# Gated attention and MLP mixer on one core: when the loads of batch 0 are issued

## The chip, the cores and the metric

The kernel runs on one core of one Trainium2 chip. The metric is the device time of one execution in microseconds. Seven runs of the kernel before took 1146.55 to 1149.58 us, with a median of 1147.07 us.

## What is computed

The sizes are 8 batches, 3008 rows, 256 columns, z with 64 columns, and an MLP mixer with 256 token features and 1536 channel features.

```python
scores = matmul(z, z.T) / S
attn   = maximum(scores, 0) ** 2
x      = u * matmul(attn, v)                     # gated attention

h  = maximum(x.T @ w_tok1, 0) @ w_tok2           # token mixing
u2 = x + h.T
out = u2 + maximum(u2 @ w_ch1, 0) @ w_ch2        # channel mixing
```

u, v, z and the weights come as float32; the kernel casts them to bfloat16 while it loads them.

## The kernel before

**Tiling.** The 3008 rows are cut into 6 groups of 512 (NG = NQ = 6; the last one holds 448). A block (b, q, g) is the scores of query group q against key group g of batch b, as four tiles of 128 keys. For a block, PE makes the scores in two units of two tiles (`score_run`, L424), ACT takes relu with the factor 1/S from PSUM into an `at` buffer (`relu`, L462), and DVE squares it there (`square`, L470). PE then multiplies v with it (`av_matmul`, L646) into two accumulators. A row is all six blocks of one q. At its end the accumulator is summed (ACT L771, DVE L777) and gated with u (DVE L798), which gives x.

**Symmetry.** The scores are symmetric, so from batch 1 on only the blocks with g >= q are computed. The block (q, g) gives (g, q) through a transpose by DMA, which SP issues (`flip`, L518, `fl<-at`). In batch 0 all blocks are computed directly, and no flip is made. There are six `at` buffers and ten `fl` buffers; the v tiles of batch 0 live in `fl` buffers too.

**Mixer.** When a batch's last row is done, its mixer is queued: `tok1` (L851), `tok2` (L870), `ch1` (L911, with w_ch1), `ch2` (L955, with w_ch2). PE does these pieces between the attention rows of the next batch. So batch 0's mixer runs in batch 1, and the weights are loaded once, before it.

**Order.** The order of every engine's instructions is made when the program is built: a planner keeps a clock for PE (`pe[0]`) and for the other engines with a cost for each operation, and picks what PE does next (scores, AV or a mixer piece) by what is ready on that clock. A load counts as ready at a time that is written beside it: `w_done[part].t` for the channel weights (L1214), `tok2_done` for w_tok2. The engines run their lists in this order and wait for one another through semaphores.

**Loads.** Loads that cast are issued by POOL: v (`load_v`, L206), u (`load_u`, L218), z (`load_z`, L125), w_tok1 (`load_w_tok1`, L236), w_tok2 (`load_w_tok2`, L246), w_ch1 and w_ch2 (`load_w_ch`, L253 and L258; two parts each). SP issues the transposes of u (L228), z (L137), x (L811) and of the flips, and the stores. `at_group(n, f)` puts f ahead of step n of the attention, a step being one block of a row; batch 0 has the steps 0 to 35, batch 1 the steps 36 to 71. In batch 0 the u and z loads have steps of their own. The other loads that the later work needs are in the list `items` (v of batch 1, w_tok1, w_tok2, w_ch), spread evenly over the steps from 7 on (L1227, L1228).

**Marks.** From batch 1 on, loads go through `ask`, which issues at most one in 4.5 us and puts a tiny POOL copy ahead of it: `after(recent[0])` (L120) copies one column of the newest tile that was squared, evacuated or summed on the planner's clock into `mark`. POOL does its list in order, so the load waits until that tile is there. In batch 0 no such copy stands ahead of the items: POOL issues them as fast as its queue lets it, except where a u load waits for its buffer.

Of the kernel before, what the change touches and what calls it, by code (L numbers as in the profile page):

```python
# [55 lines left out]
def kernel(  # L56
# [22 lines left out]
    NQ = (S + QW - 1) // QW  # L79
    NG = KT // GK  # L80
# [37 lines left out]
    def after(column):  # L118

        nc.gpsimd.tensor_copy(mark[:column.shape[0], :1], column)  # L120
# [77 lines left out]
    def load_v(b, c):  # L198
        if b == 0:

            vt = sb.tile([P, GK, D], BF16, tag="fl", name="v_sb", bufs=ROOM["fl"])
            live["fl"] += 1
        else:
            vt = sb.tile([P, GK, D], BF16, tag="v", name="v_sb", bufs=8)
        n = full_tiles[c]
        nc.gpsimd.dma_start(out=vt[:, :n, :], in_=rows_of(v[b], c))  # L206
        if n < GK:
            for r in range(2):
                nc.gpsimd.dma_start(
                    out=vt[r * TAIL:(r + 1) * TAIL, n, :], in_=last_rows(v[b]))  # L210
        vs[b, c] = vt
        v_in[b, c] = Done(pe[0] + 9.0 if b > 1 else 0.0)
        loading(LOAD)
# [37 lines left out]
    def load_w_ch(part):  # L251
        if part < 2:
            nc.gpsimd.dma_start(  # L253
                out=w_ch1_sb[:, part, :], in_=moe_w_ch1[part * P:(part + 1) * P, :])
        else:
            h = CHT // 2
            c0 = (part - 2) * h
            nc.gpsimd.dma_start(  # L258
                out=w_ch2_sb[:, c0:c0 + h, :],
                in_=moe_w_ch2.rearrange("(cc c) d -> c cc d", c=P)[:, c0:c0 + h, :])  # L260
        loading(LOAD * 1.5)
# [99 lines left out]
    pe = [0.0]  # L361
# [750 lines left out]
    def at_group(n, f):  # L1112
        fetch.setdefault(n, []).append(f)
# [3 lines left out]
    recent = [None]  # L1117
# [91 lines left out]
    w_done = [Done() for _ in range(4)]  # L1209
    tok2_done = [Done() for _ in range(NG)]  # L1210

    def ask_w_ch(part):
        load_w_ch(part)
        w_done[part].t = pe[0] + 16.0  # L1214


    W_LATER = 4

    def ask_w_tok2(c):
        load_w_tok2(c)  # L1220
        tok2_done[c].t = pe[0] + 10.0

    items = [lambda c=c: load_v(1, c) for c in vorder]
    items += [lambda c=c: load_w_tok1(c) for c in range(NG)]
    items += [lambda c=c: ask_w_tok2(c) for c in range(NG)]
    items += [lambda part=part: ask_w_ch(part) for part in range(4)]
    for k, item in enumerate(items):  # L1227
        at_group(NG + 1 + k * (NQ * NG - 2 * NG + W_LATER) // len(items), item)  # L1228

    per_batch = 0.87 * NQ * (2 + CHT // 2) + 1.35 * 4 * NQ  # L1230
    flat = NQ * NG * 1.73 + NQ * (NQ + 1) / 2 * 0.44
# [172 lines left out]
```

## Time and profile before

The profiled execution took 1147.9 us; its span, from the first to the last instruction, is 1146.1 us.

| Engine | busy us | share of the span |
|---|---|---|
| PE (matmul) | 1133.5 | 99% |
| PE (weight load) | 672.6 | 59% |
| DVE | 637.9 | 56% |
| ACT | 549.0 | 48% |
| POOL | 154.0 | 13% |

Where things stand in the span, by the timeline: attention of batch 0 to about 90 us, with the first 25 us as start-up; rows 0 and 1 of batch 1 from 89.7 to 112.9 us; tok1 of batch 0 from 112.9 us; rows 2 and 3 of batch 1 from 118.2 to 141.4 us; then the rest of batch 0's mixer (tok2 from 141.4, ch1 from 144.0, ch2 from 153.5 us) and rows 4 and 5 from 188.7 us on. The items are issued by POOL at 18.5 us (v) to 76.2 us (the last of w_ch).

How to read the profile: busy time of PE has modelled ends, so its pace is better read from the starts of matmuls. A timeline row has the start, the length, the engine, line and operation, the tiles (written, then read), the number of instructions merged, and in brackets the idle time ahead and what ended it. In a row of windows, the numbers in front of (x...) are the busy times of PE, PE's weight loads, DVE, ACT and POOL; behind them stand the granted clock, the share of the DMA engines and the GB/s. q0 is the queue of POOL's loads, q1 that of SP's DMAs.

### The profile page before, as it was taken

The page shows a single profiled execution, that of the slowest core. Times are in us where ns is not written, and L with a number is a line of the kernel's source. Part 1 is how long each engine was busy: PE and PEld are TensorE (multiplying, and loading weights), DVE is VectorE, ACT ScalarE, POOL GpSimd, SP SyncE. Part 2 cuts the span into 40 slices and gives each one's busy share as a digit, 9 for nine tenths or more (in the row PEclk, how much of TensorE's full clock was granted, in tenths as well). Part 3 has the DMA queues.
Part 4 walks back from the last instruction along what each step waited for, and adds up shares of the span by engine and source line. Part 5 has one row for each costly group of instructions (what it writes and reads, how often), then busy time and mean ns, then how long its engine had stood idle before and what let it go on. Part 6 is the DMA issues. An engine that isn't in the chain of part 4 may idle for free.

```text
span 1146.1 us, 22411 instructions
## 1 busy us (share of the span) xinstructions
PE 1133.5 (99%) x9160; PEld 672.6 (59%) x9219; DVE 637.9 (56%) x947; ACT 549.0 (48%) x699; POOL 154.0 (13%) x387
## 2 busy tenths in 40 slices
PE   8999999999999999999999999999999999999998
PEld 3455465645557566565565655665566655566666
DVE  6888454465553755537545375555644646434544
ACT  7999534374352752526525354345542554422331
POOL 3600110210111001111011100211002110000000
PEclk9999999999999999999999999999999999999999
DMA  9999954985879858899688986798967999642122
GB/s 162 178 175 237 160 120 99 193 147 118 169 121 204 160 111 157 133 196 176 109 154 135 189 174 115 150 157 174 158 128 145 169 129 177 121 102 56 51 84 65
DMA packets 468199, 164.85 MB, mean 144 GB/s; under 512 B 431936, under 2 KB 445824, under 8 KB 468096
## 3 DMA queue, kind: packets, MB, share of 16 engines
q1 hardware_dynamic: 440240, 130.72, 58.7%
q0 software_dynamic: 27344, 32.32, 20.6%
q8 instruction: 72, 1.18, 0.4%
q10 hardware_dynamic: 512, 0.38, 0.1%
q14 instruction: 31, 0.25, 0.1%
HBM read 65.40 MB, written 24.64 MB: 79 GB/s over the span
## 4 chain that ended last, share of the span: by engine, by line
PE 96%; DMA 3%; issue 0%; POOL 0%; DVE 0%; ACT 0%; SPq 0%; ACTq 0%; DVEq 0%
PE acc L646 40%; PE op L955 21%; PE hp L911 21%; PE sc L424 6%; PE a_ps L851 4%; PE h_ps L870 4%; DMA v_sb<-in_v_dram 1%; DMA fl<-at 1%; DMA zf<-in_z_dram 1%; DMA at<-at 0%; DVE h2pre L927 0%; POOL v_sb L206 0%; ACT at L462 0%; PE first_acc L563 0%; SPq L159 0%
## 5 line engine op out<-in xcount | busy, mean ns | idle before, releaser
L646 PEld LDWEIGHTS <-v_sb 64*128 64x128 bf16 x4418 | 238.8, 94 | 223.1 <-issue 4.3
L646 PE MATMUL acc<-at,v_sb 64*128 64x512 bf16 (+1 forms) x2738 | 341.8, 374 | 0.2
L925 ACT ACTIVATE h2pre<-hp 128x1024 bf16<-128x1024 f32 (+1 forms) x161 | 160.8, 1000 | 313.9 <-PE hp L911 313.6
L462 ACT ACTIVATE at<-sc 128x1024 bf16<-128x1024 f32 (+1 forms) x294 | 287.9, 1027 | 34.0 <-PE sc L424 26.7
L911 PE MATMUL hp<-xT,w_ch_sb 128*128 128x512 bf16 (+1 forms) x1106 | 254.9, 374 | 2.4
L470 DVE TENSOR_TENSOR at<-at 128x1024 bf16<-128x1024 bf16 (+1 forms) x294 | 200.6, 687 | 101.7 <-ACT at L462 98.2
L955 PE MATMUL op<-w_ch_sb,h2pre 128*128 128x256 bf16 x2208 | 251.4, 273 | 1.3 <-ACT at L462 1.0
L955 PEld LDWEIGHTS <-h2pre 128*128 128x128 bf16 x2208 | 215.4, 98 | 39.0 <-issue 3.2
L927 DVE TENSOR_SCALAR h2pre<-hp 128x1024 bf16<-128x1024 f32 (+1 forms) x127 | 153.8, 1211 | 91.6 <-PE hp L911 91.6
L646 PE MATMUL acc<-fl,v_sb 64*128 64x512 bf16 (+1 forms) x1680 | 195.0, 367 | 0.0
L911 PEld LDWEIGHTS <-w_ch_sb 128*128 128x128 bf16 x1152 | 111.8, 98 | 125.7 <-issue 4.4
L971 DVE TENSOR_TENSOR res<-op,u_sb 128x512 f32<-128x512 f32 x87 | 60.2, 691 | 153.0 <-PE op L955 152.8
L424 PE MATMUL sc<-zT 64*128 64x512 bf16 (+1 forms) x732 | 132.2, 360 | 0.2 <-ACT zT L1237 0.2
L777 DVE TENSOR_TENSOR cp<-acc,cp 128x512 f32<-128x512 f32 (+1 forms) x94 | 63.4, 675 | 101.7 <-ACT cp L771 100.6
L771 ACT COPY cp<-acc 128x512 f32<-128x512 f32 (+1 forms) x89 | 51.5, 579 | 131.2 <-PE acc L646 115.1
L450 ACT ACTIVATE at<-sc 128x512 bf16<-128x512 f32 (+3 forms) x144 | 52.1, 440 | 54.4 <-PE sc L424 53.7
L424 PEld LDWEIGHTS <-zT 64*128 64x128 bf16 x732 | 40.3, 94 | 42.2 <-issue 6.9
L798 DVE TENSOR_TENSOR xT<-cp,uT 128x512 bf16<-128x512 f32 (+1 forms) x94 | 62.4, 665 | 3.1 <-PE hp L911 1.4
L879 DVE TENSOR_TENSOR xT<-xT,h_ps 128x1024 bf16<-128x1024 bf16 (+1 forms) x48 | 55.6, 1172 | 8.6 <-PE h_ps L870 8.3
L120 POOL CAST mark<-at 128x1 f32<-128x1 bf16 x49 | 13.2, 269 | 339.4 <-DVE at L470 339.4
L499 DVE TENSOR_TENSOR at<-at 128x512 bf16<-128x512 bf16 (+3 forms) x144 | 38.1, 320 | 30.1 <-ACT at L450 28.1
L932 POOL COPY hs<-h2pre 128x128 bf16<-128x128 bf16 x48 | 15.7, 326 | 253.6 <-ACT h2pre L925 234.0
(56 smaller groups left out, 341.1 us busy)
## 6 DMA issues: line engine op xcount, KB each, us to landing
out_dram<-res SPq DMA_DIRECT2D x87, 256.0 KB, 2.3
v_sb<-in_v_dram POOLq DMA_DIRECT2D x40, 256.0 KB, 6.0
ur<-in_u_dram POOLq DMA_DIRECT2D x40, 256.0 KB, 5.2
w_tok_sb<-in_moe_w_tok_dram POOLq DMA_DIRECT2D x10, 256.0 KB, 9.3
zs<-in_z_dram POOLq DMA_DIRECT2D x35, 64.0 KB, 3.3
at<-at SPq DMA_TRANSPOSE x108, 2.4
fl<-at SPq DMA_TRANSPOSE x105, 5.3
v_sb<-in_v_dram POOLq DMA_DIRECT2D x8, 192.0 KB, 4.6
```

What stands on the lines that cost most here:

```text
L424: nc.tensor.matmul(sc[:, r, c0:c1], zT[h, k:k + P], zT[h, m + c0:m + c1], start=True, stop=True)
L462: nc.scalar.activation(view, sv, ACT.Relu, scale=inv_S)
L470: nc.vector.tensor_mul(view, view, view)
L646: nc.tensor.matmul(o, vs[blk.b, g][rows, i, dh * P:(dh + 1) * P], rhs, start=(dh, h) not in blk.begun, stop=stop, skip_group_check=True)
L777: nc.vector.tensor_add(cp[:, :W], acc[:, 0, :W], cp[:, :W])
L798: nc.vector.tensor_mul(xT[:, dh, :full * P].rearrange("p (t s) -> p t s", s=P), acc[:, :full * P].rearrange("p (t s) -> p t s", s=P), uT[: ...
L879: nc.vector.tensor_add(to, to, h[:, :, :n * P].rearrange("p h (s t) -> p h t s", t=n))
L911: nc.tensor.matmul(hp[:, r, :W], w_ch1_sb[:, dc, cc * P:(cc + 1) * P], xT[:, dc, :W], start=(dc == 0), stop=(dc == DT - 1))
L925: nc.scalar.activation(h2[:, :, :W], hp[:, :, :W], ACT.Relu)
L927: nc.vector.tensor_single_scalar(h2[:, :, :W], hp[:, :, :W], 0.0, AX.max)
L955: nc.tensor.matmul(op[:, i, :], h2, w_ch2_sb[:, cc, :], start=(cc == 0 and (i == 0 or apart)), stop=(cc == CHT - 1), skip_group_check=True)
L971: nc.vector.tensor_add(res.rearrange("p i (h d) -> p i h d", d=P), op.rearrange("p i (h d) -> p i h d", d=P), us[:, :, half * 2:half * 2 + ...
```

## The change

Two things change. The items of batch 0 now each have a mark ahead of them (`when_reached`), where a newest tile is known. And the four loads of channel weights leave the list and go to the steps 46, 48, 51 and 53, which are in batch 1, with a mark as well. With 18 items left instead of 22, the even spread over batch 0 has other steps: v at 7 to 14, w_tok1 at 16 to 23, w_tok2 at 25 to 32. The planner's time from issue to readiness of channel weights goes from 16 to 10 us.

```diff
     def ask_w_ch(part):
         load_w_ch(part)
-        w_done[part].t = pe[0] + 16.0
+        w_done[part].t = pe[0] + 10.0
 
-    W_LATER = 4
+    W_LATER = 3
 
     items = [lambda c=c: load_v(1, c) for c in vorder]
     items += [lambda c=c: load_w_tok1(c) for c in range(NG)]
     items += [lambda c=c: ask_w_tok2(c) for c in range(NG)]
-    items += [lambda part=part: ask_w_ch(part) for part in range(4)]
+    def when_reached(item):
+        if recent[0] is not None:
+            after(recent[0])
+        item()
+
     for k, item in enumerate(items):
-        at_group(NG + 1 + k * (NQ * NG - 2 * NG + W_LATER) // len(items), item)
+        at_group(NG + 1 + k * (NQ * NG - 2 * NG + W_LATER) // len(items),
+                 lambda item=item: when_reached(item))
+
+    for part, group in enumerate((46, 48, 51, 53)):
+        at_group(group, lambda part=part: when_reached(lambda: ask_w_ch(part)))
```

## The prediction

> **What bounds the kernel now.** I read the page first. Its opening rows say that PE is busy for 99% of the span. Ends of matmuls are modelled, so that alone is weak.
>
> ```profile
> span 1146.1 us, 22411 instructions
> PE 1133.5 (99%) x9160; PEld 672.6 (59%) x9219; DVE 637.9 (56%) x947; ACT 549.0 (48%) x699; POOL 154.0 (13%) x387
> ```
>
> Next the windows (length; busy time of PE, PEld, DVE, ACT, POOL; clock; DMA share; GB/s), cut where the change acts: batch 0 behind its start-up, the first four query rows of batch 1, the rest of batch 1.
>
> ```profile
> 20.00:90.00 70.00, 69.91 (x647) 36.02 (x648) 59.90 (x96) 65.07 (x73) 21.93 (x40) 1.00 1.18 179
> 90.00:144.00 54.00, 53.95 (x487) 27.94 (x483) 34.09 (x54) 37.94 (x43) 5.40 (x13) 1.00 1.04 194
> 144.00:260.00 116.00, 115.68 (x914) 69.04 (x920) 63.73 (x90) 54.89 (x67) 15.34 (x40) 1.00 0.77 140
> ```
>
> PE lacks 0.09, 0.05 and 0.32 us. The timeline of PE tests the pace by starts, not by ends:
>
> ```profile
> 98.31 1.04 PE L646 MATMUL acc<-at,v_sb 64*128 64x512 bf16 x8
> 99.17 0.40 PE L424 MATMUL sc<-zT 64*128 64x512 bf16 x2
> 99.38 1.04 PE L646 MATMUL acc<-at,v_sb 64*128 64x512 bf16 x8
> ```
>
> Ten half-height matmuls run as five pairs from 98.31 to 99.38, so one pair in 0.214 us; the planner's own figure for 512 columns (`column_time`) is 0.216. Nothing hides between the starts. The view of waits for PE names no wait at all from 24 to 260 us and 1.2 us in the rest. So the loads of batch 0, crowded as they are, cost TensorE nothing. A change of their time has about 0.5 us to win here; the 3.55 us that PE lacks in the first 24 us lie ahead of the first moved instruction.
>
> **What the change does to the program.** I compared the built instruction orders of both kernels. PE, DVE and ACT have the same instructions in the same order, so the planner's changed numbers (16 to 10 us for the channel weights, the spacing of the loads) move no matmul. POOL gets 22 more copies into `mark` and its loads in another order; SP swaps one pair of transposes in batch 1 (the turn of u goes ahead of the turn of x). PE's work is therefore unchanged, and the change can act only through a wait.
>
> **Part 1, 18 marks and loads in batch 0.** Before, POOL ran ahead of the compute until its queue or a u buffer stopped it:
>
> ```profile
> 40.29 2.12 POOL L236 DMA_DIRECT2D w_tok_sb<-in_moe_w_tok_dram  x4 [3.02 <-DMA v_sb<-in_v_dram]
> ...
> 55.77 0.57 POOL L253 DMA_DIRECT2D w_ch_sb<-in_moe_w_ch_dram  x1
> ...
> 75.39 1.67 POOL L258 DMA_DIRECT2D w_ch_sb<-in_moe_w_ch_dram  x2
> ```
>
> After, each load stands behind a mark of the newest squared score block. I dated each mark by the end of the square that it names, in the trace of before: the v loads of batch 1 leave at about 27 to 41 us, w_tok1 at 46 to 58, w_tok2 at 62 to 80. Needed: v at 89.7 us (first AV of batch 1), w_tok1 at 112.9, w_tok2 at 141.4. With the longest landing of each in the trace (15.5 us for v, 13.2 for the token weights) they are there by 57, 72 and 94 us: over 30 us early. Cost 0. Without that cover the first of them would stop PE for its lateness.
>
> Queued behind the marks on POOL are the u and z loads and the memset of xT. The z loads of batch 1 leave by 36 us, as before (34); SP begins to turn them at 42.6 behind the x of row 1, so nothing moves. u(1,1) leaves at about 75, as before (74.87). The memset moves from 77 to about 81; its xT is written at 88.4. Cost 0.
>
> The marks themselves: POOL's `mark` copies are 0.27 us in the mean and 0.19 at least, so 22 are 4 to 6 us of an engine that is idle 87% of the time. Here a rule speaks against the change. The Trainium skill ("SBUF — State Buffer", section "SBUF: two separate sides") says that a VectorE instruction with both inputs in SBUF and a GpSimd instruction that reads SBUF take a shared port as a lock, and the later one waits for the whole of the other. L470 squares `at` in SBUF, so by the rule every mark may push a square back by 0.2 to 0.6 us, together 4 to 13 us of DVE. The rows: DVE is idle for 10.1 of the 70 us, squares stay near 0.69 us beside the marks of batch 1, and it is the mark that stretches (0.51 to 0.58 instead of 0.19 us). From 30 us on a square ends over 1 us before PE takes it, so 0.2 us later costs nothing. By the rule taken at its worst, with a push of 0.6 us at the few PSUM slots that DVE frees with under 0.5 us in hand, at most 1 us. I take 0.
>
> **Part 2, relief.** From 75 to 88 us the two w_ch2 loads and SP's transposes shared the DMA engines, and the transposes of u landed 11.5 us behind their issue (2.7 when alone). That made SP late for the first flips of batch 1. After, the w_ch2 loads are gone from there, and the flips up to 109 us land perhaps 3 us earlier. The tightest user is ACT at 96.36 us: it overwrites an `at` buffer whose flip landed at 95.94, with 0.4 us in hand. It was not late, so the gain is 0; it only gets slack.
>
> **Part 3, the four channel loads in batch 1.** By the same dating they leave at about 109, 119, 124.5 and 126.5 us. First users: w_ch1 at 144.03 (L911), w_ch2 at 153.45 (L955).
>
> ```profile
> DMA to landing us min/median/max: 9.4/13.1/15.3
> ```
>
> Even 15.3 us behind the last issues gives 134 and 142: 10 and 11 us early. The skill's fit in "DMA: Bandwidth & Descriptors", section "Anatomy of one DMA" (2.0 us plus the bytes at 436 GB/s), makes 2.9 us of a load of 384 KB, and would say that it disturbs nobody for longer than that. The trace has 5.2 us for a u load of 256 KB, where the fit has 2.6, so I take the trace, with 15.3 as the upper end.
>
> The price lies elsewhere: in SP's transposes, which share the engines. From 52 to 64 us (queue, packets, MB, share):
>
> ```profile
> q0 software_dynamic: 1712, 1.73, 91.8%
> q1 hardware_dynamic: 1717, 0.42, 31.2%
> ```
>
> and from 96 to 104 us, without loads:
>
> ```profile
> q1 hardware_dynamic: 8403, 2.11, 119.3%
> ```
>
> Transposes alone make 1050 packets per us; beside loads 143, one for each packet of a load. So a load nearly stops them while it moves. How long: landings that follow one another are 1.7 us apart for w_ch1 (70.32, 71.98) and 3.1 for w_ch2 (84.76, 87.82). The flips that this hits, from SP's timeline:
>
> ```profile
> 108.73 8.25 SPq L518 DMA_TRANSPOSE fl<-at  x4
> 117.08 1.41 SPq L811 DMA_TRANSPOSE x_sb<-xT  x1
> 118.61 1.75 SPq L228 DMA_TRANSPOSE uT<-ur  x1
> 122.75 14.01 SPq L518 DMA_TRANSPOSE fl<-at  x3
> ```
>
> PE reads these flips late (batch 1's row 4 starts at 189 us). What hurries is ACT, which waits for a flip before it reuses the `at` buffer. From landing to that use I find 7.0, 6.6, 8.7 and 7.5 us for the four flips from 108.73 on, and 3.0 us for the one issued at 122.75 (landed 128.44, ACT at 131.44). The first w_ch1 load adds 1.7 us to the four, the second 1.7 to the tail of them, x and uT: covered. The flip of 122.75 is released by PE, which frees its buffer at 122.55, so an earlier SP doesn't help it. Its packets moved behind those of the u load issued at 122.11, from 125.3 to 128. The third channel load begins to move at about 126.2 (an estimate: its issue plus 1.7 us, as for that u load). About 900 of the flip's 2048 packets are through by then; the other 1150 go at about one for one, 250 in a us: 4.6 us instead of 1.1, landing at about 131.9. ACT comes to it at 131.44, and the PE matmul that takes the PSUM slot behind it has 0.3 us in hand.
>
> ```profile
> 131.44 1.73 ACT L462 ACTIVATE at<-sc 128x896 bf16<-128x896 f32 x2
> ```
>
> So PE stalls 0 to 1 us; I take 0.5. Ends: 0 if the flip is through before the load moves, 3.2 us if both w_ch2 loads pass in front of it (2 x 3.1 less 3.0). What is late next is nothing: after 134 us ACT idles until 139.75 and the next flips are for 189 us.
>
> **Sum.** Profiled execution: span 1146.1 + 1.8 around it = 1147.9. Parts 1 and 2: 0; part 3: +0.5. That gives 1148.4 on its scale. It lies 0.8 above the median of the runs (1147.07), so 1147.6 as a median.
>
> **The rivals.** *Late flips (slower).* The flip issued at 122.75 stands behind both w_ch2 loads, or the w_ch1 loads delay SP so that it isn't issued in time. It decides when the flip lands over 3.3 us later than before. Then ACT at L462, the scores and PE stop for the excess: 1.5 to 5 us, 1149 to 1152, say 1150. For it: transposes fell to a seventh of their pace beside loads. Against: 3.0 us of slack, and half of the flip is out early. Chance 0.20.
>
> *Late weights (slower).* A channel load slips past 144 or 153 us. It would take 25 us from issue to landing, against 15.3 at most; 1150 to 1157. Chance 0.04.
>
> *Relief pays (faster).* Fewer collisions in batch 0 let PE run better: bounded by the 0.5 us that PE lacks from 20 to 260 us, so 1146.6; more only if the start-up moved. Chance 0.06.
>
> *The cover holds* (forecast, 1147.1 to 1148.5): 0.70.
>
> **Chances.** A measurement of this kernel tells about 0.2% (2.3 us) from no change. Forecast: 0.69 within, 0.01 slower. Late flips: 0.05 within, 0.15 slower. Late weights: 0.04 slower. Relief: 0.04 within, 0.02 faster. Sums: 0.02, 0.78, 0.20. The range goes from the relief to the late flips short of their worst: 1146.2 to 1150.6.
>
> **What would show it.** Right: PE waits for nothing from 20 to 125 us; POOL's marks in batch 0 follow L470; w_ch landings lie before 144 and 153 us; ACT L462 waits for `fl<-at` by 1 us at most near 131 us. Wrong: an idle PE ahead of L424 or L646 between 96 and 135 us behind ACT and `fl<-at` (late flips), PEld L911 or L955 behind w_ch (late weights), squares well over 0.69 us beside marks (the lock), or a shorter start-up.

## The result and the profile after

The changed kernel takes 1156.72 us (median of 12 runs, 1155.31 to 1163.04). The kernel before took 1147.28 us beside it (30 runs, 1146.13 to 1151.79). The ratio is 1.0086 (95% interval 1.0075 to 1.0097): 9.4 us slower, where 0.5 us more was forecast and 1150.6 us was the upper end. The profiled execution took 1157.85 us. Medians and ranges here and below are of all runs; ratios and their intervals are of the runs in the fast state alone (within 1.5% of a kernel's fastest run), so the two need not agree to the last digit.

The opening rows of its page:

```profile
span 1156.1 us, 22453 instructions
PE 1136.9 (98%) x9160; PEld 674.7 (58%) x9219; DVE 638.5 (55%) x947; ACT 549.0 (47%) x699; POOL 161.6 (14%) x409
```

The span grew by 10.0 us, but PE's busy time by 3.4 only: most of the loss is PE standing still. The windows tell where, cut as before (length; busy time of PE, PEld, DVE, ACT, POOL; clock; DMA share; GB/s):

```profile
20.00:90.00 70.00, 69.92 (x645) 36.09 (x646) 59.72 (x96) 65.22 (x73) 26.58 (x54) 1.00 1.04 161
90.00:144.00 54.00, 45.29 (x410) 24.18 (x408) 31.83 (x50) 36.81 (x41) 8.91 (x22) 0.93 1.18 188
144.00:260.00 116.00, 115.68 (x914) 67.53 (x918) 57.41 (x81) 50.04 (x62) 14.46 (x39) 0.99 0.73 138
```

In batch 0, where 18 marks were added, PE lacks 0.08 us of 70 (before: 0.09). From 90 to 144 us it lacks 8.71 instead of 0.05, and the clock row drops from 1.00 to 0.93. It is one stop, by the timeline of PE:

```profile
132.31 1.03 PE L646 MATMUL acc<-fl,v_sb 64*128 64x512 bf16 x8
142.05 1.89 PE L646 MATMUL acc<-at,v_sb 64*128 64x512 bf16 x8 [8.71 <-ACT at L462]
...
145.41 3.84 PE L646 MATMUL acc<-at,v_sb 64*128 64x512 bf16 x30
...
152.64 2.76 PE L870 MATMUL h_ps<-w_tok_sb,a_sb 128*128 128x512 bf16 x11
```

The same matmuls before, where nothing stops them:

```profile
132.00 1.03 PE L646 MATMUL acc<-fl,v_sb 64*128 64x512 bf16 x8
132.86 1.03 PE L646 MATMUL acc<-at,v_sb 64*128 64x512 bf16 x8
...
141.37 2.76 PE L870 MATMUL h_ps<-w_tok_sb,a_sb 128*128 128x512 bf16 x11
```

In after, PE waits for ACT's relu of the last score tile of row 3. The eight matmuls behind the stop take 1.89 us instead of 1.03: PE came back at about half its pace. The timeline of ACT names what ACT waits for:

```profile
141.08 1.73 ACT L462 ACTIVATE at<-sc 128x896 bf16<-128x896 f32 x2 [9.22 <-DMA fl<-at]
```

It is the instruction that the prediction showed at 131.44, and it waits 9.22 us for the flip that frees its `at` buffer: the flip that was issued at 122.75 before. SP's own timeline tells when it was issued now (the length is SP's time for the issues, not the transfer):

```profile
109.24 12.79 SPq L518 DMA_TRANSPOSE fl<-at  x4
122.15 4.58 SPq L228 DMA_TRANSPOSE uT<-ur  x1
126.84 3.40 SPq L811 DMA_TRANSPOSE x_sb<-xT  x1
130.78 16.52 SPq L518 DMA_TRANSPOSE fl<-at  x3
```

The same four flips took SP 8.25 us before, and the turns of u and x 1.75 and 1.41. So SP reached the urgent flip at 130.78, 8.03 us late. The two w_ch1 loads stand in that stretch, issued by POOL at 108.50 and 119.82: the four flips took 4.5 us more beside the first, the turn of u 2.8 us more beside the second. The turn of x took another 2.0 us more, but beside a u load (issued at 122.51) and the first w_ch2 load: from 127 to 130 us the queue of the loads moved 700 packets and that of the transposes 270. What a load does to transposes is seen in the DMA view from 111 to 114 us (queue, packets, MB, share of 16 engines). Before, without a load:

```profile
q1 hardware_dynamic: 3031, 0.77, 115.1%
```

After, with the first w_ch1 load under way:

```profile
q0 software_dynamic: 117, 0.33, 81.9%
q1 hardware_dynamic: 227, 0.05, 9.0%
```

Transposes fell from 3031 packets to 227. The packets of the first w_ch1 load move from 110.7 to 114.3 us and those of the second from 121.8 to 125.3, and q1 has no packet at all in 111 to 113 and 122 to 124.

**Where the time went.** The flip is issued 8.03 us later, and takes 10.19 us to land (at 140.97) instead of 5.69, since the w_ch2 loads and two z loads move beside it. Together it is 12.5 us late, against 3.0 us of slack: PE starts again 8.88 us later relative to the matmuls ahead (9.74 us from start to start, 0.86 before). From there to the first tok2 matmul it needs 10.59 us instead of 8.51, so the half pace costs another 2.08. With 0.31 us of difference in the start-up that is 11.27 us at the tok2 matmul (152.64 against 141.37); about 1 us comes back later, where a wait of L955 for ACT of 1.0 us is gone. The span differs by 10.0.

### The profile page after: what moved, and what is told of

Read it like the earlier page. It is cut to its first block, busy times and chain, and to the rows that moved or that the text cites. A ratio compares the mean times of both kernels' runs of the same rounds, so it can differ in the third digit from the quotient of the medians.

```text
span 1156.1 us, 22453 instructions
## 1 busy us (share of the span) xinstructions
PE 1136.9 (98%) x9160; PEld 674.7 (58%) x9219; DVE 638.5 (55%) x947; ACT 549.0 (47%) x699; POOL 161.6 (14%) x409
## 4 chain that ended last, share of the span: by engine, by line
PE 97%; DMA 2%; issue 0%; DVE 0%; ACT 0%; SPq 0%; POOL 0%; ACTq 0%; DVEq 0%
PE acc L646 40%; PE op L955 21%; PE hp L911 21%; PE sc L424 6%; PE a_ps L851 4%; PE h_ps L870 4%; DMA fl<-at 1%; PE first_acc L563 1%; DMA zf<-in_z_dram 1%; DMA at<-at 0%; DMA v_sb<-in_v_dram 0%; DVE h2pre L927 0%; ACT at L462 0%; SPq L159 0%; PE up L1196 0%
## 5 line engine op out<-in xcount | busy, mean ns | idle before, releaser
L955 PE MATMUL op<-w_ch_sb,h2pre 128*128 128x256 bf16 x2208 | 251.4, 273 | 0.3 <-DVE h2pre L927 0.2
L955 PEld LDWEIGHTS <-h2pre 128*128 128x128 bf16 x2208 | 215.4, 98 | 37.9 <-issue 2.2
L777 DVE TENSOR_TENSOR cp<-acc,cp 128x512 f32<-128x512 f32 (+1 forms) x94 | 63.4, 675 | 103.3 <-ACT cp L771 102.2
L120 POOL CAST mark<-at 128x1 f32<-128x1 bf16 x70 | 21.9, 314 | 364.8 <-DVE at L470 364.8
L798 DVE TENSOR_TENSOR xT<-cp,uT 128x512 bf16<-128x512 f32 (+1 forms) x94 | 62.4, 665 | 3.1 <-PE hp L911 1.4
```

The lines of the kernel that those rows point to most:

```text
L777: nc.vector.tensor_add(cp[:, :W], acc[:, 0, :W], cp[:, :W])
L798: nc.vector.tensor_mul(xT[:, dh, :full * P].rearrange("p (t s) -> p t s", s=P), acc[:, :full * P].rearrange("p (t s) -> p t s", s=P), uT[: ...
L955: nc.tensor.matmul(op[:, i, :], h2, w_ch2_sb[:, cc, :], start=(cc == 0 and (i == 0 or apart)), stop=(cc == CHT - 1), skip_group_check=True)
```

## Experiments

The theory: channel loads in batch 1 stop SP's transposes, SP comes late to the urgent flip, ACT waits for its buffer, PE for ACT; all else of the change is free. Rivals: the marks cost; w_ch2 beside the flip is enough; w_ch1 is enough; SP's swapped pair of turns costs. Each kernel ran beside the kernel before (medians 1147.11 to 1147.50 us). The time of the profiled execution is named beside the median, since it is the one that is read.

### Marks alone

The kernel before, with a mark ahead of all 22 items, channel loads among them:

```diff
-    for part, group in enumerate((46, 48, 51, 53)):
-        at_group(group, lambda part=part: when_reached(lambda: ask_w_ch(part)))
+    items += [lambda part=part: ask_w_ch(part) for part in range(4)]
```

(shown against after; the numbers 16 and W_LATER = 4 are those of before)

> All 22 items of batch 0 get a mark, the four channel loads among them; they stay in batch 0 (at the steps of the kernel before). Theory (channel loads in batch 1 stop SP's transposes, so that one flip lands late for ACT): no cost, 1147 to 1148 us, PE without a wait from 24 to 260 us. Rival (the marks cost: POOL's copies hold up the squares of DVE): all or a good part of the 9.4 us is here, 1150 to 1157 us, with squares longer than 0.69 us on average in batch 0.

Measured: 1163.97 us (6 runs, 1157.14 to 1166.82), ratio 1.0136 (1.0110 to 1.0162). The theory said "no cost" and was wrong here; so was the rival's mechanism. The group of squares in the window from 20 to 90 us, of the kernel before, and then of after with its 18 marks (busy, mean ns):

```profile
L470 DVE TENSOR_TENSOR at<-at 128x1024 bf16<-128x1024 bf16 (+1 forms) x68 | 45.2, 676 | 9.9 <-ACT at L462 9.7
```

```profile
L470 DVE TENSOR_TENSOR at<-at 128x1024 bf16<-128x1024 bf16 (+1 forms) x68 | 45.2, 676 | 10.1 <-ACT at L462 9.9
```

A square takes 676 ns with marks and without (680 in this experiment): the marks don't stretch it. What stops PE here is read off the timelines of SP, DVE and PE, in that order:

```profile
68.81 3.52 SPq L228 DMA_TRANSPOSE uT<-ur  x1
72.42 14.48 SPq L811 DMA_TRANSPOSE x_sb<-xT  x1
```

```profile
92.70 0.69 DVE L798 TENSOR_TENSOR xT<-cp,uT 128x512 bf16<-128x512 f32 x1 [15.76 <-DMA uT<-ur]
```

```profile
94.05 0.56 PE L424 MATMUL sc<-zT 64*128 64x448 bf16 x2 [14.94 <-DVE cp L777]
```

The marks hold the last four w_tok2 loads and w_ch1 back until 66 to 74 us, where POOL issues them one behind another. SP had issued the turn of u at 68.81, but beside these loads and those issued ahead of them it landed only at 92.61, 23.8 us later; the turn of x behind it took SP 14.48 us to issue. DVE stands at the gate (L798) 15.76 us for this uT, its sums come late, and PE waits 14.94 us for a free accumulator. From 72 to 86 us the DMA view has 1503 packets of q1 beside 1468 of q0. So here transposes went on one for one with the packets of the loads, at 107 in a us, and what came late was a landing and not an issue of SP. So the theory had to be widened: not "channel loads in batch 1", but a block of loads wherever a transpose has little slack.

The same kernel once more:

> The kernel with all 22 items of batch 0 marked, once more. Theory (w_tok2 and w_ch1 leave as a block behind a full queue at 66 to 75 us and stop the transposes of x and u): again a wait of DVE for uT and of PE for a sum near 80 to 95 us, 6 to 17 us long. Rival (the wait of 14.9 us in the first profile was an accident): no PE wait there, and the loss lies elsewhere.

1164.55 us: PE waits 8.5 us for DVE L777 at the same place, and 3.9 us for an ACT that waits 4.8 us for a flip. The loss comes again, its size and split vary.

### The move alone

After, without the marks on the 18 items of batch 0:

```diff
-                 lambda item=item: when_reached(item))
+                 item)
```

> The 18 items of batch 0 have no mark, as before; the four channel loads go to the steps 46, 48, 51 and 53 with their marks, as after. Theory: all of the loss is here, 1156 to 1158 us, with one wait of PE for ACT of about 8.7 us near 133 to 142 us. Rival (marks of batch 0): 1147 to 1149 us.

Measured: 1159.94 us (6 runs, 1155.11 to 1167.95), ratio 1.0111 (1.0081 to 1.0140), which overlaps that of after. The loss is the move's; the marks of batch 0 add nothing to it. The profile has the wait of after, and smaller ones ahead of it: ACT waits for flips 1.27 us up to 113.80, 4.07 us up to 132.96 and 8.56 us up to 144.43. The flip of the second wait is one that in after landed with 0.65 us in hand.

### Only w_ch2 in batch 1

```diff
+    items += [lambda part=part: ask_w_ch(part) for part in range(2)]
 ...
-    for part, group in enumerate((46, 48, 51, 53)):
+    for part, group in ((2, 51), (3, 53)):
```

Batch 0 then has 20 items instead of 18, all with marks, so the even spread has other steps than in after.

> Only the two w_ch2 loads go to batch 1 (steps 51 and 53); the w_ch1 loads stay in batch 0 with a mark. This is the part that I costed at 0.5 us (0 to 3.2). Theory (SP's lateness, made by the w_ch1 loads, is needed): the flip of 122.75 us is issued on time and meets the w_ch2 loads half through, so 1147 to 1150.5 us. Rival (loads beside the flip are enough): the flip lands 12 us late, 1154 to 1157 us.

Measured: 1147.74 us (22 runs, 1145.83 to 1166.41), ratio 1.0024 (1.0003 to 1.0046); the profiled execution took 1146.78. In its trace the flip is issued on time and ACT doesn't wait:

```profile
122.64 15.41 SPq L518 DMA_TRANSPOSE fl<-at  x3
```

```profile
131.33 1.73 ACT L462 ACTIVATE at<-sc 128x896 bf16<-128x896 f32 x2
```

The flip landed at 130.75. So w_ch2 beside a punctual flip is about what the prediction made of it, 131.9. But ten of the 22 runs took 1153 to 1166 us. Their granted clock was 0.994 to 0.998, that of the twelve others 0.999 to 1.000. Four more executions were profiled to find out why:

> The kernel with only w_ch2 in batch 1 once more, since its single runs fell into two groups (12 of 22 at 1146 to 1148 us, 10 at 1153 to 1166). If this run is of the upper group, its trace tells where the loss lies. Theory A: in batch 0, where w_tok2 and w_ch1 stop the transposes of x and u, DVE waits for uT and PE for a sum at 75 to 95 us (as in the run with marks only). Theory B: at the flip of 122.6 us beside w_ch2, ACT waits for it near 131 us. If it is of the lower group, neither wait is there.

> The same kernel again, with the same reading: theory A a wait for uT and a sum at 75 to 95 us, theory B a wait for the flip near 131 us, or a run of the lower group without either.

> The kernel with only w_ch2 in batch 1 once more, to catch a run of the upper group (1153 to 1166 us). Theory A: a wait for uT and a sum at 75 to 95 us (transposes of batch 0 behind w_tok2 and w_ch1). Theory B: a wait of ACT for the flip of 122.6 near 131 us. A run of the lower group (1146 to 1148 us) has neither.

> The same kernel and reading as the run before it: theory A a wait for uT and a sum at 75 to 95 us, theory B a wait for a flip near 131 us, or neither at 1146 to 1148 us.

They took 1146.51, 1146.17, 1147.08 and 1146.58 us, with no wait of PE from 20 to 260 us in any of the four; the flip landed 0.3 to 0.8 us ahead of ACT. Thin slack is what they show; where the longer runs lose their time no trace here shows, and it may be in batch 0, where w_ch1 has marks as in the kernel with marks alone.

### Only w_ch1 in batch 1

```diff
+    items += [lambda part=part: ask_w_ch(part) for part in (2, 3)]
 ...
-    for part, group in enumerate((46, 48, 51, 53)):
+    for part, group in ((0, 46), (1, 48)):
```

> Only the two w_ch1 loads go to batch 1 (steps 46 and 48); the w_ch2 loads stay in batch 0 with a mark. Theory: SP falls about 8 us behind, so that the flip is issued at about 130 us instead of 122.75; with no load beside it then it lands 3 to 5 us later, at 133 to 136 us, where ACT wants it at 131.4: a PE stall of 2 to 5 us, 1149 to 1153 us. Rival (w_ch1 only delays flips with slack, as I predicted; the w_ch2 loads in front of the flip make the whole loss): 1147 to 1148 us. Rival (w_ch1 alone makes the whole loss): 1156 to 1157 us.

Measured: 1152.73 us (22 runs, 1148.78 to 1159.45), ratio 1.0045 (1.0030 to 1.0060); the profiled execution took 1150.85. The flip is issued at 128.46 and lands at 134.60; PE waits 2.9 us. As the theory had it, and the rival that is my own prediction ("covered") falls.

The same question with no channel load in batch 0:

```diff
-    for part, group in enumerate((46, 48, 51, 53)):
+    for part, group in ((0, 46), (1, 48), (2, 56), (3, 58)):
```

> The kernel after, with only the two w_ch1 loads at the steps 46 and 48 and the two w_ch2 loads behind the urgent flip (steps 56 and 58, near 134 us). No channel load is in batch 0, unlike the run with w_ch1 alone before. Theory: the w_ch1 loads make SP 6 to 8 us late with the flip of 122.75, which then lands at 133 to 137 us; PE waits 2 to 5 us and the time is 1149 to 1152 us. So about a third to a half of the loss comes by w_ch1 alone, the rest only when w_ch2 stands beside the late flip. Rival (w_ch1 makes all of it): 1156 us. Rival (w_ch1 is covered, as predicted): 1147 us.

Measured: 1152.00 us (22 runs, 1149.68 to 1171.18), ratio 1.0034 (1.0016 to 1.0052), profiled execution 1151.94. The flip is issued at 129.01 and lands at 135.31. ACT:

```profile
135.42 1.73 ACT L462 ACTIVATE at<-sc 128x896 bf16<-128x896 f32 x2 [3.98 <-DMA fl<-at]
```

By the two ratios, two w_ch1 loads make two fifths to a half of the loss; the rest needs w_ch2 beside a flip that is late already. In both kernels the flip was issued about 6 us late (5.7 and 6.3), not 8.0 as in after, where the turn of x ahead of it took 3.40 us instead of 2.0, with the first w_ch2 load beside it.

### One load ahead of the flip

This weighs the term that I had sized at 1.7 us.

```diff
-    for part, group in enumerate((46, 48, 51, 53)):
+    for part, group in enumerate((46, 53, 56, 58)):
```

> The kernel after, with one w_ch1 load ahead of the urgent flip (step 46) and the other three behind its release (steps 53, 56 and 58). It weighs the term that I sized at 1.7 us. In the run with two w_ch1 loads ahead of it, the flip of 122.5 was issued at 129.0, and SP had about 2.2 us idle before it in the kernel before: 8.7 us for two loads. Theory (4.3 us for each load, one after the other): with one load the flip is issued 4.3 less 2.2 us late, at 124 to 125.5 us, lands by 131, and PE waits under 1 us for ACT: 1147 to 1148.5 us. My figure of 1.7 us for each load: the flip is issued at 122.5 as before. Rival (only two loads together stop SP, or the loads delay it by something that doesn't add up): 122.5 or 127 and more.

Measured: 1154.08 us (7 runs, 1148.67 to 1165.86), ratio 1.0059 (1.0041 to 1.0076). In the profiled execution, which took 1148.67, the flip is issued where 4.3 us for a load put it:

```profile
124.44 17.88 SPq L518 DMA_TRANSPOSE fl<-at  x3
```

But it landed at 133.97, not by 131: the second w_ch1 load, issued at 125.98, met it. So the forecast of 1147 to 1148.5 us failed. Two more executions were profiled for the longer runs:

> The kernel with one w_ch1 load ahead of the flip once more. Its profiled run took 1148.7 us, five of its six other runs 1153 to 1155 us. Theory: in those runs the same wait of ACT for the flip is longer (6 to 8 us instead of 3.0), since the flip, issued 1.5 us ahead of the w_ch1 load of 126 us, comes through before or behind it by little differences. Rival A: another wait, in batch 0 or at L911. Rival B: no wait, but PE at a lower clock.

> The same kernel and reading as the run before it: 1153 to 1155 us with a longer wait of ACT for the flip (theory), with another wait (rival A), or with a lower clock alone (rival B).

They took 1152.45 and 1153.79 us: the flip was issued at 125.27 and 128.49, and the wait for it is longer. The second of these issues is 4 us later than one w_ch1 load explains. SP's turn of x stood ahead of it:

```profile
123.76 4.21 SPq L811 DMA_TRANSPOSE x_sb<-xT  x1
```

In the first profile it took 1.24 us. Here it met a u load issued at 122.23: from 124 to 126 us q1 moved 28 packets and q0 71. The kernel before has such a load at 122.11, but there SP's turns had landed by 122.31. So once SP is late it runs into loads that harmed nothing before.

The first AV matmuls behind the wait, of the first profile and of the last:

```profile
135.04 1.04 PE L646 MATMUL acc<-at,v_sb 64*128 64x512 bf16 x8 [2.47 <-ACT at L462]
```

```profile
137.49 1.89 PE L646 MATMUL acc<-at,v_sb 64*128 64x512 bf16 x8 [4.44 <-ACT at L462]
```

Theory held for where, not for how much: the waits are 2.5, 3.7 and 4.4 us, not 6 to 8. The rest of the difference is rival B's: behind the wait of 2.47 us PE goes on at full pace (1.04 us), behind 4.44 at half (1.89).

### All loads behind the flip's release

```diff
-    for part, group in enumerate((46, 48, 51, 53)):
+    for part, group in enumerate((53, 55, 57, 59)):
```

> The kernel after, with the four channel loads at the steps 53, 55, 57 and 59, behind the release of the urgent flip: by their marks they leave at about 128 to 135 us. Theory (channel loads hurt through the flips ahead of 123 us and the flip of 122.75 itself): this flip lands near 128.4 us as before, no PE wait of over 0.5 us, 1146.5 to 1148 us. If w_ch1 then lands past 144 us, PE waits for it at L911 by the excess, up to 3 us. Rival (any channel load in batch 1 costs, wherever it is): 1150 us or more with ACT waiting for a flip.

Measured: 1149.94 us (14 runs, 1147.66 to 1166.01), ratio 1.0013 (0.9991 to 1.0035), profiled execution 1149.39. The flip lands at 128.14 and ACT doesn't wait. But my bound of 0.5 us failed. Timelines of DVE and PE:

```profile
158.92 1.29 DVE L798 TENSOR_TENSOR xT<-cp,uT 128x512 bf16<-128x512 f32 x2 [8.40 <-PE op L955]
```

```profile
161.40 5.34 PE L911 MATMUL hp<-xT,w_ch_sb 128*128 128x512 bf16 x23 [2.52 <-DVE h2pre L927]
```

The releaser in the first row is doubtful: `op` was running all along, and the turn of u2 (L893) that reads an xT buffer landed at 158.73, 0.19 us ahead of it. SP issued that turn at 155.84 instead of 143.94, since a flip, a turn of x and one of u took it 10.43, 4.05 and 4.19 us beside these loads (before: 1.98, 1.26 and 1.26). I take this turn as the releaser; it wasn't tried by itself. Late DVE then makes PE wait at ch1 instead. The second w_ch1 load landed at 144.25, just behind its first use, which cost PE's weight loads 0.4 us.

### A seventh `at` buffer

This test takes away not the late flip but the need for it. All engines have the same order as after; room comes from one v and one res buffer.

```diff
-  ... tag="v", name="v_sb", bufs=8)
+  ... tag="v", name="v_sb", bufs=7)
-  ... tag="at", name="at", bufs=ROOM["at"])
+  ... tag="at", name="at", bufs=ROOM["at"] + 1)
-  ... tag="res", name="cp", bufs=3)
+  ... tag="res", name="cp", bufs=2)
-  ... tag="res", name="res", bufs=3)
+  ... tag="res", name="res", bufs=2)
```

> The kernel after, with the same order of instructions on every engine, but with seven at buffers instead of six (room for it from one v and one res buffer less). The channel loads and the late flips stay. The score tile that ACT fills at 131 us then reuses a buffer whose flip was issued one earlier. Theory (PE stops only because ACT waits for the buffer of the late flip): the flip of 122.75 still lands at about 135 to 141 us, but ACT doesn't wait for it, PE loses under 1 us from 112 to 144 us, and the time is 1146.5 to 1148.5 us, unless the missing v or res buffer costs in later batches (which the waits past 200 us would show). Rival (the loss comes from the loads themselves, by contention for SBUF or the clock): 1154 to 1157 us with PE slow or waiting all the same.

Measured: 1149.39 us (22 runs, 1145.94 to 1171.11), ratio 1.0023 (1.0006 to 1.0041). The profiled execution took 1146.34 us with a span of 1144.6. SP and ACT in it:

```profile
130.27 14.25 SPq L518 DMA_TRANSPOSE fl<-at  x3
```

```profile
131.29 1.73 ACT L462 ACTIVATE at<-sc 128x896 bf16<-128x896 f32 x2
```

The flip is as late as in after, and lands even later (142.94 against 140.97), ACT doesn't wait, and PE is busy for 32.00 of the 32 us from 112 to 144 (after: 23.29). The same loads, the same swapped turns, the same marks, and the stop is gone in this execution. So for the stop, contention for anything but SP's transposes, and the swap, are ruled out as causes. The other runs have no trace, but a clock: in 14 of the 22 (1145.94 to 1150.06 us) it was 0.999 to 1.000, while all 12 runs of after had 0.993 to 0.997, so a stop like that of after isn't in these 14. The median lies 0.9 us above what I expected, and eight runs took 1152 us and more at a clock of 0.991 to 0.998; what these lose, and whether a v or res buffer is behind it, stays open.

## Why the prediction was wrong

**Right: the bound, the orders, Part 1 and Part 2.** PE is the bound and PE, DVE and ACT kept their order. The 18 marks in batch 0 cost nothing (69.92 of 70 us busy); the lock rule was rightly taken at 0, since the squares stayed at 676 ns. The relief was smaller than "perhaps 3 us" (the flip with 0.4 us in hand landed 1.6 us earlier), and it gained nothing, as said. But Part 1 was free only because the channel loads had left the list: with them in it the marks cost 16 us.

**Right: the dates.** The channel loads left at 108.5, 119.8, 124.6 and 126.8 us (forecast 109, 119, 124.5, 126.5), and landed at 115.1, 125.8, 131.6 and 138.2, ahead of their uses. "Late weights" falls.

**Wrong: the step "The first w_ch1 load adds 1.7 us to the four, the second 1.7 to the tail of them, x and uT: covered."** The term measured about 4.3 us for each load: from two loads (flip issued at 129.0 in place of 122.5, plus 2.2 us for which SP had been idle), and again from one load in two of three traces (124.44 and 125.27; in the third, at 128.49, a u load had held SP up too). SP's time for the four flips says the same of the first load: 12.6 to 13.3 us in these kernels, against 8.25. I had read 1.7 us off the spacing of two landings. Those two loads moved at the same time, so their landings lie closer together than the time for which either of them occupies the engines. In the trace of before their 256 packets (3072 B each) run from 64.6 to 71.4 us, 3.4 us for each load, which would have been a better size. And I had averaged over 12 us in which transposes went on one for one; that they can stop altogether was in the trace of before too: from 94 to 95 us a u load moved 112 packets and q1 none.

**Wrong: what the SP queue carries on.** "The flip of 122.75 is released by PE, ... so an earlier SP doesn't help it" is true of an earlier SP. I didn't ask what a later one does. I had weighed the hit flips by the slack of each, and all four did hold (those with 7.0, 6.6 and 7.5 us had 3.2, 1.5 and 0.65 left). But the delay stays in SP's list, and the next flip had 3.0 us against 8.0.

**Right in kind: w_ch2 in front of the flip.** I costed this part at a landing of 131.9 us; with w_ch1 out of the way it was 130.4 to 131.5 in five traces, and harmless in these (the ten longer runs of that kernel stay open). Behind the late SP the flip took 4.5 us longer to land beside it than before.

**The rival "late flips" was the mechanism**, named with "or the w_ch1 loads delay SP so that it isn't issued in time". I gave it 1.5 to 5 us and one chance in five. Its "or" should have been an "and": about 6 us of late issue from the w_ch1 loads, 2 more once w_ch2 moves there too, and 4.5 us of longer landing, less 3.0 of slack. And "what is late next is nothing" left out that PE comes back from such a stop at half pace, for 2.1 us more.

## What to carry to other kernels

When a load moves to another stage, follow the in-order queue that shares its DMA engines to its next urgent entry: a delay adds up along the queue, and slacks are not to be weighed entry by entry. Size a load's blockade by the time over which its packets move, not by the spacing of landings, and give it a range: here it was 1.7 us by landings, 3.4 by packets and 4.3 by SP's time, and a queue that is late runs into further loads. And where a transfer has to land before a buffer is reused, one more buffer can remove the loss without moving a single load.

## What the runs showed of the hardware

- While a 384 KB load that casts was moving, transposes of 256 B packets nearly stopped: 227 packets in 3 us against 3031, and about 4.3 us of SP's time for each load. At other times they went on one for one with the packets of the loads: 1717 beside 1712 in the kernel before from 52 to 64 us, 1503 beside 1468 with marks alone from 72 to 86 us. What decides between the two was not found.
- TensorE's pace after a stop changed between stops of 2.5 and 2.9 us. From the first matmul behind the stop to the first tok2 matmul it is 8.51 us without a stop and 8.53 behind 2.5 us, but 10.22, 10.21, 10.00, 11.21 and 10.59 behind 2.9, 3.5, 3.7, 4.4 and 8.7 us. The granted clock from 112 to 144 us goes with it: 1.00 without a stop and behind 2.5 us, then 0.95, 0.95, 0.95, 0.89 and 0.88. The Trainium skill ("TensorE: Matmul & The Clock Gate", section "What's actually happening") has the clock halved after an idle window of about 3.4 us, and full again after as long a busy one, with windows that don't start with the kernel's work. The runs agree in kind; here 2.9 us (by the profile's modelled ends) was already enough. So the stops of 2.9 and 3.5 us cost 4.6 and 5.2 in all.
